# A gated FFT and MLP mixer on one core: first x block and last store in halves on two queues, two filter loads moved to GpSimd's queue

## The chip, the cores and the metric

One core of a Trainium2 chip runs the whole kernel. The metric is device time in microseconds (us), the median of several runs. The engines are TensorE (PE, with its weight loads as PEld), VectorE (DVE), ScalarE (ACT), GpSimd (POOL) and SyncE (SP). DMA transfers are issued here from three of them: SyncE, ScalarE and GpSimd; a "q" behind an engine's name in a profile row (SPq, ACTq, POOLq) is its instruction queue.

## The reference

The input x is 2048 rows (s) by 512 columns (d), bf16. Two branches are mixed by a gate per row:

```
g = sigmoid(sum_d x * gate_w)
a = irfft2( rfft2(x) * (w_r + 1j*w_i) )                 # w_r, w_i: 2048 x 257
h = layernorm over d of x
u = gelu( h^T w1 + b1 )                                  # w1: 2048 x 1792
b = (u w2 + b2)^T                                        # w2: 1792 x 2048
out = g * a + (1 - g) * b
```

## The kernel before

Rows are held as 16 blocks of 128 partitions, j = 4q + r: q is the quarter of the rows, r the residue of the row modulo 4. `x4` and `o4` are the views of x and of the output in that order; `t["x"]` is the tile `[128, q, r, 512]`. So "block 0 of x" is q = 0, r = 0.

**Stages.** (1) x, the first part of w1 and tables arrive. For each block there are statistics (VectorE's `bn_stats`, L489, or for blocks 8, 12, 5 and 2 ScalarE's sum and square, L499 and L503), then ScalarE's `rstd` (L493), then the normalised block `h` (VectorE L520 or ScalarE L550). (2) TensorE multiplies w1 by h, `m1` (L722), into 14 row tiles of u, and between them takes the forward transform along s (`fa`, L579 to L582, evicted by ScalarE at L585) and along d (`fb`, L687 and L690, evicted at L694). (3) VectorE multiplies the spectrum by the filter W (L827), and prepares single columns for it: `wprep` (L776 to L780) reads all of W, `c0a` (L790 and L791) copies one column of each half of the spectrum, `c0b` (L808 to L813) multiplies them, `nyq` (L800 to L803) does a single line. (4) TensorE multiplies w2 by gelu(u), `m2` (L988), and between those products takes the inverse transforms (L888 to L895, L970 to L974). (5) The two branches are added per pair of blocks (L993 to L1018), and for the last two blocks by L1030 straight from PSUM. Blocks are stored in groups: 0 to 3, 4 to 7, 8 to 11, 12 and 13, 14, 15. Block 15 is computed and stored in two parts of 384 and 128 columns.

**The order of work.** Every step is a task in a list, `add(engine, cost, emit, reads, writes, prio, ...)`. A planner (`Plan.order`) simulates the list with its own costs. Each time an engine is free it takes the ready task of lowest `prio`, and the tasks are emitted in the order of their planned starts; that gives each engine's instruction order. The planner reckons DMA as one stream that serves transfers in the order of issue. An issue from SyncE or ScalarE is held until the transfer eight before it has landed. `pk=(n, size, k)` gives a transfer's packets, their bytes, and how many of the 16 DMA engines take part. Tasks of the engine name "NOP" emit nothing and only carry dependencies. On the chip the instructions of an engine run in that order, each when its operands are there. All DMAs of the kernel's own helpers are issued at L317 (and the gathers at L462).

**What the change touches.**
- `ld_x0(q, eng, prio)` loads block q of r = 0 (128 rows of 1024 bytes). Block 0 goes on SyncE's queue, blocks 2, 1 and 3 on ScalarE's, ahead of ScalarE's first activation (`presq`, L372, with a table load). On SyncE the four pieces of w1 for r = 0 (`ld_w10`), the table `ta`, then x and w1 for r = 1, 2, 3 follow.
- `ld_W(comp, ...)` loads the filter, comp 0 from w_r and comp 1 from w_i, in five direct transfers and eight gathers. Transfers 0 and 1 are small and go on GpSimd's queue early. Transfers 2 (63 partitions, 252 rows of 514 bytes), 3 and 4 go on SyncE's queue behind w1. The gathers are GpSimd's; they stand behind `hold`, a copy of one element that waits for the last block of x.
- `store` writes a group; for block 15 it is called for n = 0 (384 columns) and n = 1 (128 columns).

Other steps that are spoken of: nine warm-up matmuls (L367) run on TensorE while the first data arrive; `ti` is the table of the inverse transform, loaded on GpSimd's queue behind the gathers; `wa` and `wb` are the buffers for w1 and later w2.

Of the kernel before, what the change touches and what calls it, by code (L numbers as in the profile page):

```python
# [143 lines left out]
class Plan:  # L144
# [11 lines left out]
    def add(self, eng, dur, emit, reads=(), writes=(), prio=0.0, alloc=(), free=(), pk=None, after=()):  # L156
        t = Task()
        t.eng, t.dur, t.emit, t.prio = eng, dur, emit, prio
        t.alloc, t.free, t.pk = tuple(alloc), tuple(free), pk
        t.users, t.end, t.ready = [], None, 0.0  # L160
        deps = set(after)
        for k in reads:
            if k in self.last_w:
                deps.add(self.last_w[k])
            self.readers.setdefault(k, []).append(t)
        for k in writes:
            if k in self.last_w:
                deps.add(self.last_w[k])
            deps.update(self.readers.get(k, ()))
            self.last_w[k] = t  # L170
            self.readers[k] = []
        deps.discard(t)
        t.deps = deps
        self.tasks.append(t)
        return t
# [100 lines left out]
def kernel(  # L276
# [13 lines left out]
    nc = tc.nc  # L290
    V, A, T = nc.vector, nc.scalar, nc.tensor
# [3 lines left out]
    x4 = A_x[0].rearrange(rows, q=4, r=4)  # L295
    o4 = out[0].rearrange(rows, q=4, r=4)
# [16 lines left out]
    add = pl.add  # L313
    t = {}

    def dma(out_ap, in_ap, eng=None):
        (eng or nc.sync).dma_start(out=out_ap, in_=in_ap)  # L317
# [34 lines left out]
    a0 = add("SP", 0.6, alloc_first, writes=["warm", "xs", "eps"], prio=-9)  # L352
# [7 lines left out]
    def ld(keys, dst, src, pk, prio, eng="SP"):  # L360
        return add(eng, 0.6 if eng == "POOL" else 0.43, lambda: dma(dst(), src, {"SP": None, "ACT": A, "POOL": nc.gpsimd}[eng]), writes=keys, prio=prio, pk=pk, after=[a0])
# [25 lines left out]
    def ld_x0(q, eng, prio):  # L387
        ld([("x", 0, q)], lambda q=q: t["x"][:, q, 0, :], x4[:, q, 0, :], (P, 1024), prio, eng)
# [5 lines left out]
    def ld_ta(r, prio, eng="SP"):  # L394
        ld([("ta", r)], lambda r=r: t["ta"][:, r, :], tabs["ta"][:, r, :], (P, 1280), prio, eng)

    ld_x0(0, "SP", -9)
    ld_x0(2, "ACT", -9)
    ld_w10(0, "SP", -8.9)
    ld_x0(1, "ACT", -8.9)  # L400
# [5 lines left out]
    for r in range(1, 4):  # L406
        for qs in ((slice(0, 2), slice(2, 4)) if r == 1 else (slice(0, 4),)):
            n = qs.stop - qs.start
            ld([("x", r, q) for q in range(4)[qs]], lambda r=r, qs=qs: t["x"][:, qs, r, :], x4[:, qs, r, :], (P * n, 1024), 2 * r + 0.1 * qs.start)
            add("SP", 0.43, ld_w1(r, qs), writes=[("w1", 0, 4 * q + r) for q in range(4)[qs]], prio=2 * r + 0.25 + 0.1 * qs.start,  # L410
                pk=(P * n, 1536))
# [27 lines left out]
    def ld_W(comp, pr, early):  # L439
        w = wsrc[comp]  # L440
        v = w.rearrange("(e c k) l -> c e k l", e=4, k=4)
        z = w.rearrange("(e h i n k) l -> n h k i e l", e=4, h=2, n=2, k=2)
        W = lambda: t["W"][:, comp]
        few = w.rearrange("(c b a w) l -> w c a b l", c=2, b=2, a=2)[0:1, 0]
        keys = []
        for n, (dst, src, pk) in enumerate((
                (lambda: W()[0:1, 0, :, 0, 0:257].rearrange("p (a b) l -> p a b l", a=2), few, (4, 514, 4)),
                (lambda: t["wn"][:, comp, 0:257], w[1024:1025, :], (1, 514, 1)),
                (lambda: W()[1:64, 0, :, 0, 0:257], z[0, 0, 0, 1:64], (252, 514, 9)),
                (lambda: W()[64:128, 0, :, 0, 0:257], z[1, 0, 0], (256, 514)),  # L450
                (lambda: W()[:, 1, :, 0, 0:257], v[:, :, 1, :], (512, 514)))):
            keys.append(("Wl", comp, n))
            add("SP" if n > 1 else "POOL", 0.5 if n > 1 else 0.55, lambda dst=dst, src=src, e=None if n > 1 else nc.gpsimd: dma(dst(), src, e),
                writes=keys[-1:], prio=pr + 0.1 * n if n > 1 else early + n, pk=pk, after=[a0])
        if comp == 0:
            def hold():
                nc.gpsimd.tensor_copy(t["hold"][:], t["x"][0:1, 3, 3, 0:1])
            add("POOL", 0.2, hold, reads=[("x", 3, 3)], writes=["hold"], prio=early + 19, after=[a0])
        for lt in range(2):
            for e in range(4):  # L460
                keys.append(("Wg", comp, lt, e))
                add("POOL", 1.0, lambda lt=lt, e=e: nc.gpsimd.indirect_dma_start(  # L462
                    out=W()[:, lt, e, 1, 0:257], out_offset=None, in_=w,
                    in_offset=bass.IndirectOffsetOnAxis(ap=t["ix"][:, 4 * lt + e:4 * lt + e + 1], axis=0)),
                    reads=["ix", "hold"], writes=keys[-1:], prio=early + 20, pk=(P, 514), after=[a0])
        add("NOP", 4.0, lambda: None, reads=keys, writes=[("W", comp)])
# [17 lines left out]
    for r in range(4):  # L484
# [10 lines left out]
        for n, j in enumerate(OWN[r]):  # L495
# [11 lines left out]
            else:  # L507
                add("DVE", 0.82, lambda j=j: stat(j), reads=[("x", r, j // 4)], writes=[("mv", j)], prio=pj, after=[n0] if j == 4 else ())
            sj = add("ACT", 0.28, lambda j=j: sq(t["rstd"][:, j:j + 1], t["mv"][:, j, 1:2], 1.0 / D if j in ASTAT else 1.0),
                reads=[("mv", j), "eps"], writes=[("rstd", j)], prio=-3)  # L510
# [153 lines left out]
    for lt in range(2):  # L664
        pr = 3.0 + 0.1 * lt
# [262 lines left out]
    for i in range(NW):  # L928
        n = (0, 3, 5)
# [31 lines left out]
    for grp in groups:  # L961
# [72 lines left out]
        for n, cs in enumerate(parts):  # L1034
            def store(grp=grp, cs=cs):
                q, r0, r1 = grp[0] // 4, grp[0] % 4, grp[-1] % 4 + 1
                dma(o4[:, q, r0:r1, cs], t["tb_"][:, grp[0]:grp[-1] + 1].rearrange("p j h d -> p j (h d)")[:, :, cs])
            add("SP", 0.5, store, reads=[("o", j) for j in grp] + [("of", j, n) for j in grp if j >= LATE], prio=50,
                pk=(P * len(grp), 2 * (cs.stop - cs.start)))

    order_ = pl.order()
# [33 lines left out]
```

## Time and profile before

| what | value |
|---|---|
| median of 3 runs | 130.48 us (130.34 to 130.52) |
| the profiled execution | 129.9 us, of which its span is 128.1 us |
| TensorE busy | 122.4 us, 96% of the span |
| VectorE busy | 109.9 us, 86% |
| ScalarE busy | 81.4 us, 64% |
| GpSimd busy | 26.4 us, 21% |
| granted TensorE clock | 1.0 in all 40 slices |
| DMA moved | 23.14 MB, mean 181 GB/s over the span |
| first real matmul starts | 5.17 us |
| last instruction of VectorE | 125.38 to 125.73 us |

Rows of the timeline give the start and the duration in us from the start of the span, the engine, the line of the kernel, the operation, the output and input tiles with their shapes, a count where rows were merged, and in brackets the idle time before it with what ended it. Rows of waits give who waited for whom, the total in us, how often, and the longest. Rows of DMA issues give output and input, the issuing queue, the count, the size, and the time from issue to landing. Busy time of PE is modelled: overlapping matmuls are each shown longer than the step from one to the next.

### The profile page before, as it was taken

Reading aid. Unit: us, or ns where it says so; the run is one execution under the profiler, and the core shown is the slowest. Engines: PE = TensorE matmul, PEld = TensorE weight load, DVE = VectorE, ACT = ScalarE, POOL = GpSimd, SP = SyncE. Lnnn points to the kernel's source line nnn. Section 1 sums busy time; section 2 is a strip of 40 time slices with the busy share of each in tenths; the row PEclk is TensorE's granted clock in tenths of the full one; section 3 lists DMA queues with packets and bytes.
Section 4 is the critical chain, followed back from the end, with each engine's and each line's share of the span. In section 5 each row is a group of like instructions: output and inputs, shape, how many; then the busy total and the mean of one; then the engine's idle time right before and its main releaser. Section 6 shows DMA issues by size and latency. Waiting matters only on the chain.

```text
span 128.1 us, 2101 instructions
## 1 busy us (share of the span) xinstructions
PE 122.4 (96%) x745; PEld 69.4 (54%) x759; DVE 109.9 (86%) x242; ACT 81.4 (64%) x170; POOL 26.4 (21%) x35
## 2 busy tenths in 40 slices
PE   6999889999999999999999999999999999999991
PEld 2455345655444467754445545556875676655570
DVE  2796989999999999889999999999586489999832
ACT  3879679797997899978220046225995599842200
POOL 5970005778978500000000000000000000000000
PEclk9999999999999999999999999999999999999999
DMA  3999999999999999980008800000000001243031
GB/s 102 345 333 383 319 394 382 352 339 338 257 188 214 347 409 411 416 338 26 0 0 298 360 0 0 0 0 10 0 0 0 0 5 67 97 164 155 14 123 41
DMA packets 15027, 23.14 MB, mean 181 GB/s; under 512 B 1464, under 2 KB 12106, under 8 KB 15018
## 3 DMA queue, kind: packets, MB, share of 16 engines
q1 hardware_dynamic: 13338, 19.70, 46.1%
q0 software_dynamic: 1200, 2.91, 7.4%
q10 hardware_dynamic: 480, 0.40, 0.9%
q8 instruction: 6, 0.10, 0.3%
q14 instruction: 3, 0.02, 0.1%
HBM read 20.90 MB, written 2.10 MB: 180 GB/s over the span
## 4 chain that ended last, share of the span: by engine, by line
PE 82%; DMA 11%; ACT 2%; issue 1%; ACTq 1%; SPq 0%; DVE 0%
PE acc L988 37%; PE acc L722 27%; DMA x<-in_A_x_dram 11%; PE fb L722 3%; PE fb L690 1%; PE fb L888 1%; PE fa L888 1%; PE fa L690 1%; PE fa L581 1%; PE fa L582 1%; ACTq L317 1%; ACT gl L503 1%; PE fa L988 1%; PE fa L579 1%; PE fb L687 1%
## 5 line engine op out<-in xcount | busy, mean ns | idle before, releaser
L988 PE MATMUL acc<-gl,wb 128*128 128x512 bf16 (+1 forms) x124 | 31.9, 376 | 0.2
L722 PE MATMUL acc<-h,wb 128*128 128x512 bf16 x124 | 28.9, 379 | 0.1
L988 PE MATMUL acc<-gl,wa 128*128 128x512 bf16 (+1 forms) x93 | 23.5, 376 | 0.1
L988 PEld LDWEIGHTS <-wb 128*128 128x128 bf16 x136 | 14.6, 114 | 10.6 <-issue 0.2
L1004 ACT ACTIVATE x<-acc,ombb,omg 128x512 bf16<-128x512 f32 x14 | 10.7, 780 | 14.6 <-PE acc L988 14.6
L722 PEld LDWEIGHTS <-wb 128*128 128x128 bf16 x128 | 12.5, 98 | 13.6
L722 PE MATMUL acc<-h,wa 128*128 128x512 bf16 (+1 forms) x66 | 16.8, 369 | 0.8 <-DMA wa<-in_B_w_dram 0.5
L988 PEld LDWEIGHTS <-wa 128*128 128x128 bf16 x102 | 11.2, 113 | 8.6
L722 PEld LDWEIGHTS <-wa 128*128 128x128 bf16 x102 | 9.9, 99 | 9.9 <-DMA wa<-in_B_w_dram 1.6
L742 ACT ACTIVATE gl<-acc,b1f 128x512 bf16<-128x512 f32 x12 | 8.1, 698 | 7.2 <-PE acc L722 7.2
L489 DVE BATCH_NORM_STATS2 stats<-x 128x6 f32<-128x512 bf16 x12 | 8.2, 686 | 3.1 <-DMA x<-in_A_x_dram 3.1
L758 ACT ACTIVATE x<-x 128x512 bf16<-128x512 bf16 x16 | 10.0, 637 | 0.0
L585 ACT CAST X<-fa 128x512 bf16<-128x512 f32 x16 | 8.8, 576 | 1.4 <-PE fa L582 1.4
L462 POOL DMA_INDIRECT W<-in_A_w_i_dram,ix x8 | 9.2, 1150 | 2.4 <-issue 2.4
L722 PE MATMUL fb<-h,wa 128*128 128x512 bf16 (+1 forms) x33 | 9.5, 366 | 0.0
L462 POOL DMA_INDIRECT W<-in_A_w_r_dram,ix x8 | 8.6, 1070 | 2.3 <-issue 2.3
L550 ACT ACTIVATE h<-x,nmr,rstd 128x512 bf16<-128x512 bf16 x8 | 6.5, 810 | 0.3 <-DVE nmr L547 0.3
L978 ACT ACTIVATE X<-fa,g 128x512 bf16<-128x512 f32 x8 | 5.7, 711 | 1.3 <-PE fa L974 1.3
L859 ACT CAST s<-fa 8x512 bf16<-8x512 f32 x1 | 0.6, 575 | 8.3 <-PE fa L857 8.3
L978 ACT ACTIVATE X<-fb,g 128x512 bf16<-128x512 f32 x8 | 5.7, 718 | 0.0
L694 ACT CAST B<-fa 128x512 bf16<-128x512 f32 x8 | 5.0, 630 | 0.2 <-PE fa L690 0.2
L694 ACT CAST B<-fb 128x512 bf16<-128x512 f32 x8 | 5.0, 626 | 0.0
(178 smaller groups left out, 244.1 us busy)
## 6 DMA issues: line engine op xcount, KB each, us to landing
wb<-in_B_w_dram SPq DMA_DIRECT2D x8, 512.0 KB, 9.8
wb<-in_B_w_dram SPq DMA_DIRECT2D x4, 1024.0 KB, 7.7
wa<-in_B_w_dram SPq DMA_DIRECT2D x3, 1024.0 KB, 11.3
wa<-in_B_w_dram SPq DMA_DIRECT2D x2, 768.0 KB, 11.6
out_dram<-x SPq DMA_DIRECT2D x3, 512.0 KB, 2.9
x<-in_A_x_dram SPq DMA_DIRECT2D x2, 512.0 KB, 11.8
wa<-in_B_w_dram SPq DMA_DIRECT2D x4, 192.0 KB, 3.8
wa<-in_B_w_dram SPq DMA_DIRECT2D x2, 384.0 KB, 6.5
```

The costliest lines, as they stand in the source:

```text
L462: add("POOL", 1.0, lambda lt=lt, e=e: nc.gpsimd.indirect_dma_start(out=W()[:, lt, e, 1, 0:257], out_offset=None, in_=w, in_offset=bass.Ind ...
L489: V.bn_stats(out=t["stats"][:, j, :], in_=t["x"][:, j // 4, j % 4, :])
L550: add("ACT", act(512, 2), lambda j=j: A.activation(t["h"][:, j // 4, j % 4, :], t["x"][:, j // 4, j % 4, :], ActF.Identity, bias=t["nmr"][ ...
L585: add("ACT", act(512), lambda r=r, dq=dq: A.copy(t["X"][:, :, r, :, dq, :], t["pa", r, dq][:]), reads=[("pa", r, dq)], writes=[("X", r, dq ...
L690: T.matmul(pb[:, :, 1::2, :], lhsT=w(k), rhs=tbl(k, c), start=(k == 2), stop=(k == 3))
L694: A.copy(t["B"][:, lt, e, 2 * c:2 * c + 2, :].rearrange("p s (i b) -> p s i b", b=4), t["pb", lt, e, c][:].rearrange("p s b i -> p s i b"))
L722: T.matmul(t["u", ft][:, cs], lhsT=w[:, j // 4, j % 4, c * P:(c + 1) * P], rhs=t["h"][:, j // 4, j % 4, cs], start=(j == jorder[0] and not ...
L742: gelus.append(add("ACT", act(512, 1), lambda ft=ft: A.activation(t["gl"][:, ft, :], t["u", ft][:], ActF.Gelu_apprx_tanh, bias=t["b1f"][:, ...
L758: A.activation(t["x"][:, q, r, :], t["x"][:, q, r, :], ActF.Copy, accum_out=t["glog"][:, 4 * q + r:4 * q + r + 1])
L978: A.activation(epair(j // 2 % NEO)[:, j % 2], t["i3", j][:], ActF.Copy, scale=t["g"][:, j:j + 1])
L988: T.matmul(t["y", j, n][:, cs], lhsT=w[:, o, 512 * q + r:512 * q + 512:4], rhs=t["gl"][:, ft, cs], start=(ft == 0), stop=(ft == NFT - 1))
L1004: A.activation(tbuf(j).rearrange("p h d -> p (h d)"), t["y", j, 0][:], ActF.Identity, bias=t["ombb2"][:, j:j + 1], scale=t["omg"][:, j:j + 1])
```

## The change

Block 0 of x is loaded in two transfers of 64 partitions, the first on SyncE's queue and the second on ScalarE's, both ahead of everything else there; a NOP task joins them. The third direct filter transfer (n = 2) of each component goes on GpSimd's queue instead of SyncE's, behind `hold`: for w_r between `hold` and its gathers, for w_i between the gathers of w_r and those of w_i. The store of block 15's last 128 columns is issued in two transfers of 64 partitions, the first from ScalarE and the second from SyncE.

```diff
-    ld_x0(0, "SP", -9)
+    for n, eng in enumerate(("SP", "ACT")):
+        ps_ = slice(64 * n, 64 * n + 64)
+        ld([("x0", n)], lambda ps_=ps_: t["x"][ps_, 0, 0, :], x4[ps_, 0, 0, :], (64, 1024), -9.1, eng)
+    add("NOP", 0.0, lambda: None, reads=[("x0", 0), ("x0", 1)], writes=[("x", 0, 0)])
     ld_x0(2, "ACT", -9)
     ld_w10(0, "SP", -8.9)
...
         keys = []
+        if comp == 0:
+            def hold():
+                nc.gpsimd.tensor_copy(t["hold"][:], t["x"][0:1, 3, 3, 0:1])
+            add("POOL", 0.2, hold, reads=[("x", 3, 3)], writes=["hold"], prio=early + 19, after=[a0])
...
-            add("SP" if n > 1 else "POOL", 0.5 if n > 1 else 0.55, lambda dst=dst, src=src, e=None if n > 1 else nc.gpsimd: dma(dst(), src, e),
-                writes=keys[-1:], prio=pr + 0.1 * n if n > 1 else early + n, pk=pk, after=[a0])
-        if comp == 0:
-            def hold():
-                nc.gpsimd.tensor_copy(t["hold"][:], t["x"][0:1, 3, 3, 0:1])
-            add("POOL", 0.2, hold, reads=[("x", 3, 3)], writes=["hold"], prio=early + 19, after=[a0])
+            add("SP" if n > 2 else "POOL", 0.5 if n > 2 else 0.55, lambda dst=dst, src=src, e=None if n > 2 else nc.gpsimd: dma(dst(), src, e),
+                reads=["hold"] if n == 2 else (), writes=keys[-1:], prio=pr + 0.1 * n if n > 2 else early + (19.5 if n == 2 else n), pk=pk, after=[a0])
...
-            add("SP", 0.5, store, reads=[("o", j) for j in grp] + [("of", j, n) for j in grp if j >= LATE], prio=50,
+            def store2(grp=grp, cs=cs):
+                q, r = grp[0] // 4, grp[0] % 4
+                for lo, eng in ((0, A), (64, None)):
+                    dma(o4[lo:lo + 64, q, r, cs], t["tb_"][lo:lo + 64, grp[0]].rearrange("p h d -> p (h d)")[:, cs], eng)
+            add("SP", 0.5, store2 if n == 1 else store, reads=[("o", j) for j in grp] + [("of", j, n) for j in grp if j >= LATE], prio=50,
                 pk=(P * len(grp), 2 * (cs.stop - cs.start)))
```

## The prediction

> **What bounds the kernel now.** I read the engine shares first, then who waited for whom on TensorE, then the order of time at three places: the start, the filter product, the end.
>
> ```profile
> PE 122.4 (96%) x745; PEld 69.4 (54%) x759; DVE 109.9 (86%) x242; ACT 81.4 (64%) x170; POOL 26.4 (21%) x35
> PE fa L367 <- DVE eps L329: 1.0, 1, 1.0
> PE acc L722 <- DMA wa<-in_B_w_dram: 0.5, 1, 0.5
> PE fa L579 <- ACT X L585: 0.5, 1, 0.5
> ...
> 5.17:20.00 14.83, 13.72 (x83) 7.57 (x84) 13.05 (x36) 11.56 (x33) 3.70 (x7) 1.00 1.04 361
> 20.00:66.00 46.00, 45.68 (x275) 24.82 (x280) 43.96 (x103) 37.57 (x86) 18.94 (x18) 1.00 0.88 273
> ```
>
> The first line is the page, the next three are all of TensorE's waits, the last two are busy time by stretch (span, then PE, PEld, DVE, ACT, POOL, then clock, DMA share, GB/s). After its warm-up TensorE waits twice: 0.5 us at 15.47 for a piece of w1, and 0.5 us at 19.40 for an eviction that stands behind the x block landing at 16.80. Up to 20 us the 16 DMA engines are full (share 1.04, 361 GB/s). From 20 on TensorE is full at clock 1.00. So the end is: DMA stream up to 19.40, a fixed queue of matmuls to 125.4, then a tail.
>
> The start, and the tail (start, duration, what; the DMA rows end in KB and us to landing):
>
> ```profile
> 2.15 1.28 ACT L372 ACT_TABLE_LOAD   x1 [2.15 <-issue]
> 3.41 0.69 DVE L489 BATCH_NORM_STATS2 stats<-x 128x6 f32<-128x512 bf16 x1 [1.84 <-DMA x<-in_A_x_dram]
> 3.65 0.61 ACT L499 ACTIVATE gl<-x 128x512 f32<-128x512 bf16 x1
> 4.36 0.29 ACT L493 ACTIVATE rstd<-mv,eps 128x1 f32<-128x1 f32 x1
> ...
> 122.32 0.75 DVE L1030 SCALAR_TENSOR_TENSOR x<-acc,omg,x 128x512 bf16<-128x512 f32 x1 [1.12 <-PE acc L988]
> 124.59 0.62 DVE L1030 SCALAR_TENSOR_TENSOR x<-acc,omg,x 128x384 bf16<-128x384 f32 x1 [1.53 <-PE acc L988]
> 125.38 0.35 DVE L1030 SCALAR_TENSOR_TENSOR x<-fa,omg,x 128x128 bf16<-128x128 f32 x1 [0.17 <-PE fa L988]
> out_dram<-x SPq DMA_DIRECT2D x1, 96.0 KB, 1.6
> out_dram<-x SPq DMA_DIRECT2D x1, 32.0 KB, 1.5
> ```
>
> ScalarE holds three x loads ahead of its table load; block 0 of x reaches VectorE at 3.41, its rstd runs at 4.36, the first real matmul at 5.17. At the end VectorE waits for TensorE, twice over a microsecond: it has slack. The last store is issued at 125.75, lands at about 127.25, and 0.85 us of closing follow to 128.1.
>
> **Part 1, block 0 of x in halves.** The first slice of 3.2 us moved 102 GB/s, 326 KB, the next ran at 345 GB/s, so data flows from about 3.2 - 326/345 = 2.25 (estimate). Today blocks 0 and 2 (262 KB) go side by side: through at 3.01, seen by VectorE 0.40 later. With only block 0 in front (131 KB) it is seen at 2.63 + 0.40 = 3.03; the other end is no gain, 3.41. ScalarE now issues four loads instead of three, 0.46 each: table load at 2.61, the first instruction after presq at 4.11 (3.65 + 0.46). VectorE's statistics take 0.95 (3.41 to 4.36), so rstd of block 0 can run at max(3.98, 4.11) = 4.11, if it goes ahead of block 8's sum (L499). In the planner's order it does, since block 2 of x moves behind half of block 0. From rstd to matmul takes 0.81: 4.92, but the nine warm-up matmuls end at 5.02. Gain: 0.15. In the old order of ScalarE rstd would stand at 4.82: a loss of 0.46. I take the gain.
>
> Behind it block 8 is later: sum from 4.31, square 5.05, rstd 5.88 (0.83 after, as today), normalised 6.21 to 6.61, matmul 6.7 against 6.65 now. TensorE's twelve half matmuls (1.48) end at 6.50, so 0.2 is lost again. Sum at 6.7: +0.05, bounds -0.15 and +0.46. All of it goes into the 0.5 us wait at 15.47, which the DMA stream sets. With that cover gone it would count in full.
>
> Does the stream move? Same bytes, same order on SyncE. Tile's transfers wait for the one eight before (w1's fourth piece starts at 3.59, 0.56 after ta: it waits for x). One more in front puts ta under that wait, 2.60 to about 3.1, and what follows up to 0.4 later; three w1 pieces (576 KB, 1.6 us) are then queued, so no engine runs dry. By bounds: 64 KB less ahead on SyncE's own queue, -0.18; the issue lag in full, +0.4. Taken: 0, as the stream is full.
>
> The Trainium skill speaks against this part: "DMA: Bandwidth & Descriptors", section "Rules for kernel authors", says that transfers to disjoint partition halves serialize on the same engines and one whole transfer should be used. By it block 0 would be seen at 3.41 as now and the 0.15 would fall away; the sum at the end stays.
>
> **Part 2, the filter loads.** GpSimd: hold ends at 20.71; two direct loads at 0.54 to 0.61 each (its rows), with up to the 0.30 that stands between its gathers: 1.1 to 1.8 us for what is queued behind, 16 gathers and the ti load. The last gather, issued at 42.24, landing 7.3 later at 49.5, comes at 50.6 to 51.3; VectorE first uses W at 54.31. Cover 3.0. The ti load moves from 43.22 to at most 45.0, lands 8.2 later, 53.2; TensorE reads it at 88.23. SyncE drops two transfers between 26.91 and 36.61, so w2 starts up to 3 us earlier, and is not used before 66.21. The 126.5 KB burst at 20.7 costs other loads 0.35 us: w1's last piece lands near 22.6 and is used after 24.3, the first wb loads land near 29.7 and are used at 33.31.
>
> What does move is VectorE's order, because the planner charges gathers issued behind w2 with w2's bytes. Worked through by hand, the filter counts as ready some 2 to 3 us later in its reckoning, and c0a of the second half (L790) slips in directly behind wprep. That copy needs the last spectrum eviction:
>
> ```profile
> 54.31 0.41 DVE L776 TENSOR_SCALAR W<-W 1x1028 bf16<-1x1028 bf16 x1
> 55.33 0.16 DVE L808 TENSOR_TENSOR cm<-c,wpm 128x8 f32<-128x8 f32 x1
> 58.06 0.15 DVE L790 CAST c<-B 128x8 f32<-128x8 bf16 x1
> 56.64 0.58 ACT L694 CAST B<-fb 128x512 bf16<-128x512 f32 x1
> ```
>
> The eviction ends at 57.22, so VectorE would stand from 55.4 to 57.25: a hole of 1.9. TensorE fills with the second layer's matmuls (L988), which need none of it; the inverse transform moves back with the plan. Tail: VectorE's own work for rows 14 and 15 ends at 119.30 and 120.59 and with it at 122.5; one L1018 (0.69) brings 123.2, L1030 of row 14 (0.75) 123.95, and row 15's is due at 124.59. Cover left: 0.65. Cost taken: 0; bounds 0 and +0.6 (hole one microsecond larger, then spread over the slack of 0.17 and up at each L1030).
>
> **Part 3, the last store.** 96 KB land in 1.6, 32 KB in 1.5: 64 KB are 0.1, so 16 KB save about 0.03. SyncE issues stores in 0.33; at the start ScalarE's issues took 0.41 to 0.45 beside SyncE's 0.39 to 0.43. Its half may land 0.02 to 0.12 later. Bounds -0.1 and +0.15; taken -0.03, nearest to the size rows.
>
> **Sum:** 0 + 0 - 0.03. The profiled execution took 129.9 (span 128.1 and 1.8 around it), 0.58 below the median of 130.48; its difference is carried over: 130.45.
>
> **The rivals.** *Slower: the hole outgrows its cover.* If the planner puts c0a even ahead of wprep (in its reckoning the two lie half a microsecond apart), the hole is 57.25 - 54.31 = 2.9. It decides from 2.6 on. Row 14's L1030 ends near 124.95, the next two follow 0.2 to 0.4 late, and its 128 KB store lies beside the last ones: +0.3 to +0.6, about 130.9. For it: VectorE at 86%. Against it: 1.1, 1.5 and 2.2 us waits of VectorE in the tail.
> *Faster: the early stream lands earlier.* If x and w1 on SyncE's queue gain the 64 KB (0.18) and both waits of TensorE shrink by that, with 0.1 at the store: -0.28, 130.2. For it: 1.0 us of TensorE's waiting hangs on that stream. Against it: share 1.04.
> *The change does not do what it says:* halves that share the engines arrive together with what they displaced, and 130.5 stays. It lies inside the forecast.
>
> **How the numbers follow.** Forecast, no change that counts: 0.42 (0.12 of it the last rival). Slower 0.31: 0.18 the hole, 0.13 the early order of ScalarE or the store's second queue past their covers. Faster 0.27. About 0.2% (0.26 us) is what a measurement of this kernel can tell from no change. The range goes from 129.9 (the faster rival with the store's bound and one full wait of 0.5) to 131.1 (the slower one at its upper price). The forecast's own range is 130.2 to 130.7.
>
> **What would show it.** Right: L489 first at about 3.05, the table load at 2.61, the first L722 near 5.0, a wait at 15.4 for wa and at 19.4 for ACT as now, L790 second pair before L808 with a wait of about 1.9, PE's last matmul near 125.3, stores landing near 127.2. Wrong: TensorE waiting anywhere after 20; L1030 of row 15 behind row 14's; the L722 start at 5.6; the x landing at 16.8 shifted by 0.3 or more.

## The result, and the profile after

The changed kernel took 131.39 us (median of 12 runs, 130.62 to 131.90), the kernel before in the same comparison 129.63 us (12 runs, 128.98 to 130.52). The paired ratio is 1.0119, 95% interval 1.0090 to 1.0148: 1.54 us slower, bounds 1.17 and 1.92 (the ratio times 129.6; the two medians differ by 1.76). The execution that was profiled took 130.62 us (span 128.8), the shortest of its twelve; so its trace shows only 0.7 of the 1.54 us, and the rest has to be looked for in the experiments. Five runs below (e5_store_act, e6_store_sp2, e7_x0_cols, e8_x0_sp2, e15_x0_merge) fell on chips that lowered the clock in some or all of their executions, and what is used of their times is from undisturbed executions alone.

Engine shares and all waits of TensorE, after (page, then chain of waits):

```profile
PE 122.5 (95%) x745; PEld 69.6 (54%) x759; DVE 110.3 (86%) x242; ACT 81.1 (63%) x170; POOL 28.7 (22%) x37
```
```profile
PE fa L367 <- DVE eps L329: 1.0, 1, 1.0
PE acc L725 <- DVE h L523: 0.8, 2, 0.4
PE fa L582 <- ACT X L588: 0.4, 2, 0.2
```

TensorE has the same work to 0.1 us, and its waits after the warm-up now sum to 1.2 instead of 1.0. But they lie elsewhere: 0.8 stand at the start (VectorE's `h`), 0.4 behind the eviction that was seen at 19.4 before. The wait for w1 at 15.47 is gone. The start, in order of time (start, duration, engine, what, and what it waited for):

```profile
0.75 2.45 ACTq L317 DMA_DIRECT2D x<-in_A_x_dram  x4
...
3.23 1.28 ACT L372 ACT_TABLE_LOAD   x1 [3.23 <-issue]
...
3.38 0.69 DVE L492 BATCH_NORM_STATS2 stats<-x 128x6 f32<-128x512 bf16 x1 [1.80 <-DMA x<-in_A_x_dram]
...
4.73 0.28 ACT L496 ACTIVATE rstd<-mv,eps 128x1 f32<-128x1 f32 x1
4.91 0.61 ACT L502 ACTIVATE gl<-x 128x512 f32<-128x512 bf16 x1
...
5.44 1.01 PE L725 MATMUL acc<-h,wa 128*128 128x256 bf16 x4 [0.42 <-DVE h L523]
...
6.46 0.69 DVE L492 BATCH_NORM_STATS2 stats<-x 128x6 f32<-128x512 bf16 x1 [0.79 <-DMA x<-in_A_x_dram]
6.50 0.29 ACT L496 ACTIVATE rstd<-mv,eps 128x1 f32<-128x1 f32 x1
...
7.29 0.40 DVE L523 TENSOR_SCALAR h<-x,mv,rstd 128x512 bf16<-128x512 bf16 x1
...
7.74 1.02 PE L725 MATMUL acc<-h,wa 128*128 128x512 bf16 x4 [0.41 <-DVE h L523]
```

Block 0 of x is seen at 3.38, where it was 3.41. ScalarE's four issues fill 2.45 us, where three took 1.37; the table load stands at 3.23 instead of 2.15, the first matmul at 5.44 instead of 5.17, the 512-wide matmuls of block 8 at 7.74 instead of 6.65.

Two things make block 8 late. ScalarE starts later, so block 8's rstd runs at 6.50 (5.39 before). And VectorE has the statistics of block 4 ahead of block 8's `h`: they waited 0.79 us for block 4's x, up to 6.46 (5.20 before, without a wait), and `h` follows them at 7.29 (6.03 before). By the trace's records of the transfers' semaphores block 8's x landed at 4.68 (3.57 before) and block 4's at 6.44 (4.90): each stands one place further back on ScalarE's queue.

The transfers themselves start later (busy by stretch; the last columns are clock, DMA share and GB/s):

```profile
2.00:3.00 1.00, 1.00 (x4) 0.30 (x2) 0.00 (x0) 0.84 (x1) 1.00 (x3) 1.00 1.04 271
...
0.00:16.00 16.00, 14.25 (x70) 6.90 (x72) 11.73 (x34) 11.43 (x28) 7.47 (x17) 1.00 0.89 296
```
```profile
2.00:3.00 1.00, 1.00 (x4) 0.30 (x2) 0.00 (x0) 0.00 (x0) 1.00 (x3) 1.00 0.82 157
...
0.00:16.00 16.00, 13.95 (x67) 6.88 (x69) 11.50 (x33) 11.23 (x28) 7.50 (x17) 1.00 0.88 285
```

From 2 to 3 us 157 GB/s were moved instead of 271, and over the first 16 us 285 instead of 296 (294 to 306 in the profiles below whose start is that of the kernel before). On SyncE's queue `ta` is issued at 3.37 (2.60 before), the next x transfer at 4.69 (3.96):

```profile
3.37 0.33 SPq L317 DMA_DIRECT2D rot<-dft_ta  x1
3.75 0.43 SPq L317 DMA_DIRECT2D wa<-in_B_w_dram  x1
4.69 0.90 SPq L317 DMA_DIRECT2D x<-in_A_x_dram  x2
```

The filter product and the tail on VectorE, with the last store's half on ScalarE's queue:

```profile
55.39 0.17 DVE L793 CAST c<-B 128x8 f32<-128x8 bf16 x1 [1.00 <-ACT B L697]
55.88 0.17 DVE L794 CAST c<-B 128x8 f32<-128x8 bf16 x1 [0.32 <-ACT B L697]
55.99 0.42 DVE L779 TENSOR_SCALAR W<-W 1x1028 bf16<-1x1028 bf16 x1
```
```profile
122.92 0.74 DVE L1033 SCALAR_TENSOR_TENSOR x<-acc,omg,x 128x512 bf16<-128x512 f32 x1
...
124.66 0.62 DVE L1033 SCALAR_TENSOR_TENSOR x<-acc,omg,x 128x384 bf16<-128x384 f32 x1 [0.99 <-PE acc L991]
...
125.44 0.35 DVE L1033 SCALAR_TENSOR_TENSOR x<-fa,omg,x 128x128 bf16<-128x128 f32 x1 [0.16 <-PE fa L991]
125.83 0.57 ACTq L317 DMA_DIRECT2D out_dram<-x  x1
```
```profile
out_dram<-x ACTq DMA_DIRECT2D x1, 16.0 KB, 2.1
```

The two copies c0a (L793, L794) went ahead of wprep (L779) and waited 1.32 us for the eviction; wprep runs 1.68 us later than before. The tail has absorbed it: row 14 is 0.6 later, row 15 starts at 124.66 where it was 124.59, and still waits 0.99 for TensorE. The last VectorE instruction ends 0.06 later than before (125.79 against 125.73). What follows it, to the end of the span, took 3.05 us instead of 2.39: the store's half took 0.57 to issue and 2.1 to land, where one store of 32 KB took 0.33 and 1.5.

### The profile page after: what moved, and what is told of

The parts are those of the page before. It is cut to its first block, busy times and chain, and to the rows that moved or that the text cites. A ratio compares the mean times of both kernels' runs of the same rounds, so it can differ in the third digit from the quotient of the medians.

```text
span 128.8 us, 2103 instructions
## 1 busy us (share of the span) xinstructions
PE 122.5 (95%) x745; PEld 69.6 (54%) x759; DVE 110.3 (86%) x242; ACT 81.1 (63%) x170; POOL 28.7 (22%) x37
## 4 chain that ended last, share of the span: by engine, by line
PE 82%; DMA 11%; ACT 2%; ACTq 1%; issue 1%; DVE 0%
PE acc L991 37%; PE acc L725 26%; DMA x<-in_A_x_dram 11%; PE fb L725 3%; PE fb L891 1%; ACTq L317 1%; PE fa L693 1%; PE fa L891 1%; PE fb L693 1%; PE fa L584 1%; PE fa L585 1%; ACT gl L506 1%; PE fa L991 1%; PE fa L582 1%; PE fb L690 1%
## 5 line engine op out<-in xcount | busy, mean ns | idle before, releaser
L465 POOL DMA_INDIRECT W<-in_A_w_r_dram,ix x8 | 9.4, 1181 | 2.4 <-issue 2.4
```

## The experiments

Every kernel below is the kernel before with only the edit shown. Ratios are paired with runs of the kernel before on the same chip; a per cent is 1.3 us.

**One part at a time.** The edits are the three hunks of the change.

e1_x0, the halves of x block 0 alone. Expected:

> Only block 0 of x in halves; filter and store as before. Theory A (the start carries most of the loss: ScalarE holds four issues, the changed kernel's trace shows 0.60, 0.86, 0.44 and 0.44 instead of 0.46 each, so the table load is 1.1 us later, block 8's matmuls are 1.1 us later, and the 0.5 us wait for the DMA stream hides only part): +0.6 to +1.0 us, table load near 3.2, first real matmul near 5.4. Theory B (the DMA stream hides all of the start, as predicted): within 0.2 us. The profiled pair of traces, whose last VectorE instruction is only 0.06 us later, speaks for B; the medians, which differ by 1.5 us where this pair of executions differs by 0.7, for A.

e2_store, the halves of the last store alone. Expected:

> Only the last store in halves on ScalarE's and SyncE's queues. Theory A (a transfer of 64 partitions issued beside another costs more to issue and lands later: 0.57 instead of 0.33 and 2.1 instead of 1.5 us in the changed kernel's trace): +0.5 to +0.7 us, all after the last VectorE instruction. Theory B (my prediction): within 0.15 us.

e3_filter, the filter loads alone. Expected:

> Only the third filter transfer of each component on GpSimd's queue. Theory A (VectorE's later wprep is covered by the slack of 0.6 us at the end, and the transfers are off the path): within 0.2 us, wprep near 56.0 and behind the second c0a, TensorE without a wait after 20. Theory C (the filter is the hidden loss, in executions other than the profiled one): +0.4 to +1.0 us, seen as a late L1030 for block 14 or 15.

Measured: e1_x0 131.03 us, ratio 1.0087 (1.0053 to 1.0120); e2_store 131.00, 1.0089 (1.0055 to 1.0123); e3_filter 130.09, 1.0019 (0.9995 to 1.0042). Parts 1 and 3 each cost about 1.1 us, more than theory A gave either of them, and part 2 nothing that this comparison can tell from zero. e3's VectorE order is not the one that its own expectation gave but the one that the prediction had worked out by hand (wprep, the first copy, then a wait):

```profile
54.80 0.41 DVE L776 TENSOR_SCALAR W<-W 1x1028 bf16<-1x1028 bf16 x1
...
55.87 0.17 DVE L790 CAST c<-B 128x8 f32<-128x8 bf16 x1
57.74 0.17 DVE L791 CAST c<-B 128x8 f32<-128x8 bf16 x1 [1.69 <-ACT B L694]
```

The wait was 1.69, and L790 and L791 of the second half are behind wprep; in the whole change they are ahead of it. Neither order moved the end measurably.

In e1's profiled execution TensorE waited more than in the kernel after:

```profile
PE fa L582 <- ACT X L588: 1.7, 2, 1.0
...
PE acc L725 <- DVE h L523: 0.9, 2, 0.5
```

x's third residue (ScalarE's fourth sum) was there at 18.03 instead of 16.80. This execution is the longest of e1's nine (131.88), and such figures vary without any change at the start: in the kernel before and in e2, e3, e4 and e5b, whose start is the same, the third residue came at 16.61 to 17.29, the waits behind the warm-up sum to 1.0 to 2.3, and the last matmul starts at 124.92 to 125.61. e1 lies outside with 18.03, 2.6 and 126.68; the kernel after (16.76, 1.2, 125.19) does not.

e13_x0_store, parts 1 and 3 together (both hunks as in e1 and e2). Expected:

> The change without its filter part. If the parts add: +1.7% (0.9 and 0.9), which would mean that the filter part gains 0.5% in the company of the others. If all three are near the 1.2% of the change with the filter at 0 to 0.2%: +1.0 to +1.3%.

Measured: 131.80, 1.0162 (1.0121 to 1.0203). The two parts add: 0.87% and 0.89%. It also leaves the whole change, 1.0119, below its two costly parts, by 0.4% with some 0.5% of uncertainty; whether the filter loads give anything back in company stays open, and the next finding takes away part of the difference.

**What the store pays for.** Four ways of writing the last 32 KB:

```diff
 e4_store_cols   2 x (128 partitions x 64 columns), ScalarE and SyncE
 e5_store_act    1 x (128 x 128), on ScalarE's queue
 e6_store_sp2    2 x (64 partitions x 128 columns), both on SyncE
-                for lo, eng in ((0, A), (64, None)):
-                    dma(o4[lo:lo + 64, q, r, cs], t["tb_"][lo:lo + 64, grp[0]]...[:, cs], eng)
+                for c, eng in ((cs.start, A), (cs.start + 64, None)):            # e4
+                    dma(o4[:, q, r, c:c + 64], t["tb_"][:, grp[0]]...[:, c:c + 64], eng)
+                dma(o4[:, q, r, cs], t["tb_"][:, grp[0]]...[:, cs], A)           # e5
+                for lo, eng in ((0, None), (64, None)):                          # e6
```

> The last store in two transfers on the same two queues, but of 128 partitions and 64 columns each instead of 64 partitions and 128 columns. If two queues issuing at the same moment is what costs, the issue is again near 0.57 and the loss as in the run with the store alone (+0.5 to +0.7 us). If the 64 partitions are what costs, the issues are near 0.33 to 0.4 and the time is within 0.2 us of before.

> The last store whole, in one transfer of 128 partitions, but on ScalarE's queue instead of SyncE's. Theory P (64 partitions are what costs: the column halves issued in 0.37 and 0.33 and landed in 1.6, the partition halves in 0.54 to 0.57 and 1.8 to 2.1): issue near 0.37, tail after VectorE's last instruction 2.4 to 2.8 us as with one store on SyncE, time within 0.2 us of before. Theory Q (a store on ScalarE's queue costs in itself, which would explain why the column halves were still 0.5% slower): tail 2.8 us or more, +0.4 to +0.7 us.

> The last store in two transfers of 64 partitions, both on SyncE's queue, ScalarE's left alone. Theory P: each issue near 0.55, one behind the other, so the second starts 0.6 us late and lands late: +0.8 to +1.2 us, tail 3.2 us or more. Theory Q: issues near 0.33, +0.2 to +0.4 us.

> Once more the last store whole on ScalarE's queue. Theory P (64 partitions cost, not the queue): within 0.3 us of before, issue near 0.37, tail 2.4 to 2.8 us. Theory Q: +0.4 us or more.

Measured: e4_store_cols 130.57, 1.0052 (1.0022 to 1.0081). e5_store_act 0.9955 (0.9901 to 1.0008); repeated as e5b_store_act 129.68, 1.0009 (0.9983 to 1.0034). e6_store_sp2 1.0107 (1.0052 to 1.0163); its two issues took 0.58 and 0.59, one behind the other. The landings of ScalarE's part in e4, e5b and, for comparison, e2:

```profile
out_dram<-x ACTq DMA_DIRECT2D x1, 16.0 KB, 1.6
```
```profile
out_dram<-x ACTq DMA_DIRECT2D x1, 32.0 KB, 1.5
```
```profile
out_dram<-x ACTq DMA_DIRECT2D x1, 16.0 KB, 1.8
```

ScalarE's queue costs nothing (e5b: issue 0.37, landing 1.5). Two transfers cost little at the landing, as long as each has 128 partitions (e4: 1.6). The 64 partitions do: from the issue to the moment at which SyncE's wait for the landing passes, the trace has 1.48 us before, 1.44 in e4 (SyncE's part; ScalarE's landed 1.58 after its issue), 1.51 in e5b, and 2.07 in e2, 2.07 after, 2.08 in e13 (the later of the two halves). By the records of the packets the first data packet leaves 0.83 after the issue before and in e4, but in the kernel after 1.22 after the issue for one half and 1.49 for the other.

Why then is e4 0.5% slower? Its trace gives the larger part of the answer. At the end SyncE waits for the transfers' semaphores, two in an instruction, in a fixed order; the views leave semaphore instructions out, so these rows are from the trace's records (start in us, what SyncE waits for):

```
before                        e1_x0 (whole store, split x)   after
126.13  S114, S113            127.69  S114, S113             126.43  S114, S113
126.20  S99,  S112            128.79  S99,  S112  <- store   126.49  S99,  S112
126.26  S101, S111            128.85  S101, S111             126.56  S101, S111
126.32  S103, S110            128.91  S103, S110             126.62  S103, S110
126.38  S104, S109            128.97  S104, S109             126.68  S104, S109
126.44  S105, S108            129.03  S105, S108             126.74  S105, S108
126.50  S106, S107            129.10  S106, S107             126.97  S106, S107
126.87  S116, S100            129.15  S115, S100             127.90  S115, S100  <- store
127.23  S117, S115  <- store  129.22  S116, S117             127.96  S116, S117
128.11  end                   130.10  end                    128.84  end
```

The transfers of SyncE's and ScalarE's queues take eight semaphores in turn. The kernel before has 48 of them, and the last store has the eighth, whose wait is the last of the list: the others have run out while the store was in flight. With 49 (e1, e2, e4, e6, e7, e8, e14) it, or one half of it, has the first, S99, and seven waits of 0.06 stand behind it: 0.43 us that have nothing to do with how a transfer is cut. From the last wait of the list to the end of the span it is 0.88 in all three. The whole change has 48 again (one more for x, one more for the store, two filter loads fewer) and pays 0.06. So the single parts e1 and e2 look 0.43 us worse than they are in company: about 0.70 us (1.13 - 0.43) and 0.73 (1.16 - 0.43), of which the landing explains 0.59. e4 needs 1.87 from the issue to the last wait of the list, 0.39 more than before; 0.68 - 0.39 = 0.29 is left, which its interval (0.29 to 1.05, less the 0.39) no longer tells from zero. e3, with 46, pays 0.12; e13, with 50, whose halves have S101 and S99, pays 0.43.

**What the x halves pay for.** The same pieces of x block 0 in other forms:

```diff
-        ps_ = slice(64 * n, 64 * n + 64)
-        ld([("x0", n)], lambda ps_=ps_: t["x"][ps_, 0, 0, :], x4[ps_, 0, 0, :], (64, 1024), -9.1, eng)
+        cs_ = slice(256 * n, 256 * n + 256)                                       # e7: 128 partitions x 256 columns
+        ld([("x0", n)], lambda cs_=cs_: t["x"][:, 0, 0, cs_], x4[:, 0, 0, cs_], (P, 512), -9.1, eng)
-    for n, eng in enumerate(("SP", "ACT")):
+    for n, eng in enumerate(("SP", "SP")):                                        # e8: 64-partition halves, both on SyncE
```

> Block 0 of x in two transfers on SyncE's and ScalarE's queues as in the change, but of 128 partitions and 256 columns each. Theory S (the loss is a DMA stream that starts late: in the second from 2 to 3 us it moved 157 and 162 GB/s with the partition halves, 271 to 289 without; x and w1 then land later, and the matmuls with them): with quick issues (0.40 to 0.46) the stream starts as before, 250 GB/s or more from 2 to 3 us, table load near 2.6, time within 0.3 us of before. Theory T (the loss is ScalarE's fourth issue, which makes the table load and block 8 late): +0.4 to +1.0 us with the table load still late.

> Block 0 of x in two transfers of 64 partitions, both on SyncE's queue; ScalarE has its three loads as before. Theory S: SyncE's issues are near 0.55 to 0.6 each, w1 starts 0.7 us later, the stream is slow from 2 to 3 us (below 240 GB/s), and the time is +0.4 to +1.0 us although the table load is back at 2.15. Theory T: with the table load at 2.15 the time is within 0.2 us of before.

> Once more block 0 of x in column halves of 128 partitions on the two queues, since all executions of its first try ran at a granted clock of 0.95 to 0.98 and can't be compared. That profile's start can be read: issues of 0.39 and 0.46, table load at 2.64, first matmul at 4.88, but only 176 and 180 GB/s in the two microseconds from 2 to 4 (rows of 512 bytes). Theory S (the late stream is the loss): +0.4 to +1.0 us although the first matmul is early. Theory T (the late table load): within 0.3 us of before.

> Once more block 0 of x in halves of 64 partitions, both on SyncE's queue, for the same reason. Its profile showed issues of 0.6 each, the table load at 2.14, and 295 then only 134 GB/s from 2 to 4 us. Theory S: +0.7 to +1.5 us. Theory T: within 0.3 us, unless block 0 itself comes so late (statistics at 5.3) that its matmuls are late: then up to +1 us by either, with TensorE's waits before 9 us telling which.

The first tries (146.11 and 142.19 us) say nothing of the time. Repeated: e7b_x0_cols 130.85, 1.0074 (1.0042 to 1.0106); e8b_x0_sp2 132.77, 1.0217 (1.0153 to 1.0281). ScalarE's start in e7b:

```profile
0.75 1.86 ACTq L317 DMA_DIRECT2D x<-in_A_x_dram  x4
...
2.64 1.28 ACT L372 ACT_TABLE_LOAD   x1 [2.64 <-issue]
...
5.06 0.63 ACT L502 ACTIVATE gl<-x 128x512 f32<-128x512 bf16 x1 [0.52 <-DMA x<-in_A_x_dram]
...
7.46 1.02 PE L725 MATMUL acc<-h,wa 128*128 128x512 bf16 x4 [0.37 <-DVE h L523]
```

With 128 partitions the four issues take 1.86, 0.46 each, and the table load stands at 2.64: what the prediction had worked out for the halves (2.61). SyncE's first packet leaves at 1.77, as before (1.79); with 64 partitions it is 2.11 to 2.13, in e1, e13 and the kernel after. So the 64-partition form costs issue time and 0.34 us ahead of the first byte. But e7b gains nothing by that: block 8's own x is not there before 5.06, and its matmuls start at 7.46 all the same. Of e7b's 0.96 us, 0.43 are the closing list and another 0.16 stand between the list and the end; the 0.37 left, with 0.4 of uncertainty, decides for neither theory. In e8b, where no queue but SyncE's changes, ScalarE is early (table load 2.14), and block 0 is late:

```profile
5.47 0.69 DVE L492 BATCH_NORM_STATS2 stats<-x 128x6 f32<-128x512 bf16 x1 [3.89 <-DMA x<-in_A_x_dram]
...
7.14 1.01 PE L725 MATMUL acc<-h,wa 128*128 128x256 bf16 x4 [2.12 <-DVE h L523]
```

Two halves on one queue were together at 5.47, 2.1 us later than whole. By the records of the semaphores the first half landed at 3.62 and the second, issued at 1.39, at 5.37. It stood second on SyncE's queue, where the kernel before has w1's first piece, which was issued at 1.19 and landed at 4.67: a second place costs that much without halves too. e8b's loss, 2.8 us, is above both theories; TensorE, which waits for nothing behind this point, worked at half pace up to 12.84 (last section), and that adds to it.

**Which of the two delays counts, ScalarE's start or the stream?** Two kernels were meant to move only ScalarE's start, two only the stream. e10_act_late puts two loads of 128 x 16 bytes, which nothing uses, on ScalarE's queue behind its three; e11_act_only puts four copies of 128 columns, which nothing uses, behind ScalarE's first activation and changes no transfer.

```diff
+    for n in range(2):                                                            # e10
+        ld([("scr", n)], lambda n=n: t["scr"][:, 8 * n:8 * n + 8], x4[:, 0, 0, 0:8], (P, 16), -8.87, "ACT")
     def presq():
         A.activation(t["ombb2"][:, 0:1], t["eps"][:], ActF.Abs_reciprocal_sqrt, ...)
+        for _ in range(4):                                                        # e11
+            A.copy(t["gl"][:, 0, 0:P], t["warm"])
```

> The kernel before with two extra tiny loads (128 rows of 16 bytes into a scratch tile, 4 KB in all) on ScalarE's queue between its x loads and its table load: the table load moves from 2.15 to about 3.05, as in the change, and the byte stream stays. Theory S: within 0.3 us of before (block 8's matmuls late, hidden in the waits for the stream). Theory T: +0.6 to +1.0 us.

> The kernel before with four copies of 128 columns on ScalarE behind presq (of zeros, into a place that is overwritten later): ScalarE's first sum starts about 0.9 us later (near 4.6 instead of 3.65), no transfer and no order is changed. Theory T (the late ScalarE is the loss of block 0's halves): +0.6 to +1.0 us. Theory S (the late stream is): within 0.3 us, block 8's matmuls 0.5 to 0.9 us later, and the waits near 15 and 19 us shorter by as much.

e10_act_late: 131.32, 1.0130 (1.0077 to 1.0183). It is confounded: the second tiny load was issued only at 3.52, when the transfer eight before it (block 8's x) had landed, so the table load came at 3.88 and not at 3.05; two more transfers also held SyncE's issues back, with 210 and 206 GB/s from 6 to 8 us, and the closing list cost 0.37. e11_act_only: 130.83, 1.0076 (1.0047 to 1.0105), with the stream as before (299 GB/s from 2 to 3 us, 298 over 16) and no wait of TensorE but one:

```profile
PE acc L724 <- DVE h L522: 1.3, 1, 1.3
```
```profile
3.66 1.27 ACT L374 COPY gl<-xp 128x128 bf16<-128x128 bf16 x4
...
4.96 0.63 ACT L501 ACTIVATE gl<-x 128x512 f32<-128x512 bf16 x1
...
6.30 1.01 PE L724 MATMUL acc<-h,wa 128*128 128x256 bf16 x4 [1.27 <-DVE h L522]
...
7.24 0.40 DVE L522 TENSOR_SCALAR h<-x,mv,rstd 128x512 bf16<-128x512 bf16 x1
...
8.81 1.62 PE L724 MATMUL acc<-h,wa 128*128 128x512 bf16 x4
```

ScalarE 1.3 us late puts block 8's matmuls at 8.81, 2.16 later than before; the waits that stood after them (1.0) are gone, and 2.16 - 1.0 = 1.16 is the span's increase (129.2 - 128.1 = 1.1). So a late ScalarE alone can lead to a loss of this size, but in e11 it has help that the kernel after has not: block 8's `h` was ready at 7.64 (the row at 7.24), no later than there (7.69), and TensorE took it only 1.17 later, still working through block 0's matmuls at half pace (last section). Without that, as an estimate from these rows, 2.16 - 1.17 = 0.99 would have been left, no more than the 1.0 of waits covers.

The other way round, take bytes off the early stream. GpSimd loads `tb`, `gw` and `tg` (582 KB) at 7 to 9 us. e9_defer puts all three behind `hold` (20.12 before), e12_defer2 only `gw` and `tg` (288 KB). The lines of e12, with `load` taught to pass `reads` on:

```diff
-    load("gw", [P, D], BF16, gate_w[None, :].to_broadcast([P, D]), (P, 1024), prio=28.3, eng="POOL")
+    load("gw", [P, D], BF16, gate_w[None, :].to_broadcast([P, D]), (P, 1024), prio=29.3, eng="POOL", reads=[("x", 3, 3)])
...
-    load("tg", [P, 642], BF16, tabs["tg"], (P, 1284), prio=60, eng="POOL")
+    load("tg", [P, 642], BF16, tabs["tg"], (P, 1284), prio=60, eng="POOL", reads=[("x", 3, 3)])
```

> The kernel before with three loads of GpSimd's queue (tables tb and tg and the gate weights gw, 582 KB) moved from about 8 us to behind hold, at 20 us and later. Theory S: 582 KB at 361 GB/s are 1.6 us of stream ahead of x and w1; block 2 of the third residue lands about 1 us earlier than 16.8, TensorE's wait at 19.4 shrinks, and the time is -0.4 to -1.0 us. Theory T: the start of ScalarE is unchanged, so within 0.2 us.

> The kernel before with only gw and tg (288 KB) moved behind hold on GpSimd's queue; the bias table tb stays early. Theory S: 288 KB at 361 GB/s are 0.8 us of stream, the x block of the third residue lands near 16.0 instead of 16.6 to 17.3, TensorE's wait at 19.4 mostly goes: -0.4 to -0.8 us. Theory T: within 0.2 us.

e9_defer: 130.90, 1.0104 (1.0043 to 1.0166). x's third residue is there at 14.55, 2.25 earlier, but TensorE's bias product (L701) needs `tb` and stands at 31.61 instead of 22.65:

```profile
PE acc L722 <- ACT gl L742: 2.4, 1, 2.4
```

The gain turned into a new wait. e12_defer2: 128.25, 0.9890 (0.9852 to 0.9927), 1.4 us faster than the kernel before and so the best here. x's third residue is there at 15.06, and of TensorE's waits only the one ahead of the warm-up is left:

```profile
PE fa L367 <- DVE eps L329: 1.0, 1, 1.0
```

This bears out the prediction's first reading: 1.0 us of waits hung on the early stream, and without them the end comes down by as much or more (1.4, bounds 0.9 and 1.9).

e14_x0_on_defer puts e1's hunk on e12's kernel, where no wait is left for a late start to hide in. Expected:

> The kernel with the two late GpSimd loads (gw and tg moved behind the hold, 1.1% faster than before), and on top of it the first block of x as two 64-partition halves. In that kernel TensorE waited for nothing after its start, so there is no slack left for a late start to hide in. Theory (the halves start block 8's matmuls 0.8 to 1.5 us later, and the waits of 1.0 us after them covered part of it): the lateness now counts in full, 1.0 to 1.5 us over that kernel, a ratio to before of 0.997 to 1.001. Rival (the loss is the slower stream alone, and the start is covered by something else): with x(2) already landing about 2 us earlier the halves cost at most 0.3 us, a ratio of 0.989 to 0.992.

130.02, 1.0024 (0.9996 to 1.0051): 1.0024 / 0.9890 is 1.35% or 1.75 us more than e12. The closing list has 0.43 of it, and 1.3 is left, against 0.70 for the same halves on the kernel before. The rival falls; but the 1.3 and the 0.70, with 0.6 and 0.4 of uncertainty, are not told apart, so that the cover is not shown by them. Nor does the run part the two delays as it was meant to: in its profiled execution (131.68, the longest of its twelve) x's third residue came at 17.32, 2.26 later than in e12, with 1.6 us of waiting for it.

e15_x0_merge keeps the halves and joins two of w1's first pieces, so that there are as many transfers in front as before:

```diff
-    ld_w10(2, "SP", -8.8)
-    ld_w10(1, "SP", -8.7)
+    add("SP", 0.4, ld_w1(0, slice(1, 3)), writes=[("w1", 0, 4), ("w1", 0, 8)], prio=-8.8, pk=(2 * P, 1536), after=[a0])
```

> The x halves alone, and two of w1's first pieces (for x blocks 1 and 2, 192 KB each) joined into one transfer, so that the number of transfers in front is that of before again. A transfer waits for the one eight before it, and with the halves the one that waits first (ta) was issued at 3.37 us instead of 2.60, the next x transfer at 4.69 to 5.30 instead of 3.96. Theory (one more transfer in front holds the stream back): ta is issued at 2.6 to 2.9, the following x transfer at 4.0 to 4.4, x's third residue lands near 16.8, TensorE waits at most 0.6 us for the eviction behind it. ScalarE stays late (table load at 3.2, block 8's matmuls near 7.5), and the ratio to before falls from 1.0087 to 1.003 to 1.006. Rival (the 64-partition transfers themselves hold the stream back, whatever their number): the issues on SyncE stay 0.7 us or more late, the third residue lands after 17.4, and the ratio stays at 1.007 to 1.011.

Its time (145.85 us) is of no use, so the ratios that were expected stay untested. But the granted clock is 1.0 from 4.46 to 35 us, and the start can be read:

```profile
2.45 0.47 SPq L317 DMA_DIRECT2D rot<-dft_ta  x1
3.36 0.33 SPq L317 DMA_DIRECT2D wa<-in_B_w_dram  x1
3.73 1.93 SPq L317 DMA_DIRECT2D x<-in_A_x_dram  x2
```

`ta` is issued at 2.45, the next x transfer at 3.73: a little earlier than before (2.60 and 3.96) and than the theory had it, where e1 has 3.29 and 5.08. In e1 the issue of `ta` carries a wait for the semaphore of ScalarE's half of block 0, which landed at 3.27; in e15 it carries none. So it is the number of transfers that held SyncE's `ta` back (a transfer waits for the one eight before it). The second x transfer is late still, 5.29 (4.92 before): it waits for block 8's x, which landed at 5.27. The other effect stays: 160 GB/s from 2 to 3 us (e7b, with whole partitions and half rows, has 196), table load at 3.20, block 8's matmuls at 7.69; x's third residue came at 17.12, between theory and rival and within what an unchanged start gives. With 48 transfers the last store is again the last of the closing list, and 0.88 lie between the list and the end.

## Why the prediction was wrong, step by step

It said 130.45, no change, with a range up to 131.1, and had everything on the path as covered or nil; 131.39 was measured. Its reading of the bound holds: waits at the start, a fixed queue of TensorE, a tail. Three terms were mis-sized: ScalarE's start with what follows it up to block 8, the stream, and the store. ScalarE's issues and the store rest on one assumption, that half a transfer costs no more to issue and to land than a whole one.

- **Part 1, ScalarE's issues and block 8.** Taken as 0.46 for one more; the halves made it 1.08 (0.60 and 0.86 for the first two, 0.44 for the others). The order of ScalarE that it chose came true, with rstd ahead of block 8's sum, at 4.73 instead of 4.11. "Block 0 seen at 3.03" was wrong: 3.38 (and data flows from 1.79 before, by the packets, not from 2.25). The chain "sum from 4.31 ... normalised 6.21" left out two things: when the x of blocks 8 and 4 lands, one place further back on ScalarE's queue (4.68 and 6.44, where it was 3.57 and 4.90), and that VectorE has block 4's statistics ahead of block 8's `h`. The gain of 0.15 was a loss of 0.27 at the first matmul; block 8's matmuls came at 7.74 and not 6.7, a term of +1.09 instead of +0.05, over twice its upper bound of 0.46. The nearest rival is "early order of ScalarE past its cover", which had 0.13 together with the store; but it was not the order that failed.
- **Its cover.** It was put at 0.5, the wait at 15.47; the waits came to 1.0. In the profiled execution 0.6 of them went, and TensorE's queue behind block 8 took 0.4 less (no row was found for that; at 27 us the matmuls of both kernels stand at the same time, 26.97 and 27.00), so the 1.09 did not reach the end. In the executions profiled of e1, e13 and e14 it did: behind block 8 TensorE still waited 1.7, 0.7 and 1.6, since the stream that makes these waits is later too (third residue at 18.03, 17.48 and 17.32).
- **"No engine runs dry … taken: 0, as the stream is full."** `ta` was worked out for 3.1 and issued at 3.37, and what follows 0.7 to 1.1 late (after, e1) instead of "up to 0.4". The engines were at 157 to 171 GB/s from 2 to 3 us in all kernels with the 64-partition halves on two queues (269 to 299 with the whole block), and x's third residue came at 16.76 to 18.03 (16.61 to 17.29 with an unchanged start). e1 has 1.7 us of waiting where 0.5 stood; e4, with an unchanged start, has 1.8 there, so this figure alone proves nothing.
- **Part 3, the landing.** Worked out from sizes alone at -0.03, bounds -0.1 and +0.15; it measures +0.59 at the landing. The size rows (96 KB 1.6, 32 KB 1.5) say nothing of the number of partitions, and that is what was halved. ScalarE's queue, which the prediction suspected, is free (e5b).
- **Part 2** was right: 0, with the hole on VectorE of the predicted kind (1.69 in e3 against 1.9), the last gather issued at 44.68 instead of 42.24 within its cover, and the tail's slack taking it up. In the whole change c0a went ahead of wprep, the slower rival's order; its price didn't come, since the hole was 1.32 and not 2.9, and VectorE still waited 0.99 for TensorE at row 15.
- **The Trainium skill's rule** that two transfers to disjoint partition halves serialize and aren't worth it ("DMA: Bandwidth & Descriptors", section "Rules for kernel authors") was cited and got 0.12, as the last rival. By it the 0.15 would have fallen away, and the trace agrees (3.38 against 3.41); its advice was right by more than it says, since the halves were not merely useless but cost issue and landing time.
- **Not in the prediction at all:** the closing list. In the change it is worth 0.06; in experiments that take one part alone it is worth 0.43, and would have been read as the part's price.

Added up: landing 0.59, list 0.06, x halves 0.70 (e1 less its list), filter 0.13 (e3 less its list, not told from zero) make 1.48, against 1.54 measured (1.17 to 1.92); the x halves and the filter carry some 0.4 and 0.3 of uncertainty, so that the close fit is in part luck. How the 0.70 divides between ScalarE and the stream is not settled. In the execution profiled of the kernel after, an estimate from the rows: had block 4's x been there, block 8's rstd (6.50 to 6.79) would have let its matmuls start near 7.25, so 0.6 of the 1.09 are ScalarE's start and 0.5 the stream. In e1, e13, e14 and e15 block 8's own x landed at 5.06 to 5.68, when ScalarE was already free. The stream's lateness has two causes (the number of transfers for SyncE's later issues, the form for the first microsecond).

## What to carry to other kernels

Price a transfer by its partitions and its place in the queue, not by its bytes, and ask of everything that moves back a place when it lands: look in the trace for a transfer of the same form, and if there is none, say so and take a wide bound. A wait that covers a delay covers it only if the delay doesn't also move what made the wait; ask that of every cover. And when one part of a change is tested alone, count the transfers: a part that changes their number can move a cost at the other end of the kernel, so compare the closing as well as the stage.

## What the runs showed of the hardware that was not expected

- A transfer of 64 partitions takes longer to issue than one of 128: 0.56 to 0.60 for x and 0.54 to 0.59 for the store, against 0.39 to 0.41 and 0.33 to 0.37; the issue behind it on ScalarE took 0.69 to 0.86 (0.44 before). Its first packet leaves 0.34 to 0.39 later, and that of the store's second half 0.66.
- TensorE starts at half pace, and the moment at which it goes to full pace differs from execution to execution. The "granted clock 1.0 in all 40 slices" of the page hides it: the trace has no clock record before 5.55 us in the kernel before and 6.34 in the kernel after, and where there is none the views print 1.00. Up to the first record 512-wide matmuls (the nine of the warm-up) follow one another by 0.43 us and 256-wide ones by 0.21; behind it by 0.215 and 0.11. The first record stands at 10.01 in e11 and at 12.84 in e8b, after 1.27 and 2.12 us without work, and at 3.81 to 6.97 in all others. An idle stretch does not do it alone: in e10, where the record (3.93) came ahead of 1.69 us without work, the twelve 256-wide matmuls behind them ran at full pace, 0.11 each; in e11 they took 2.51 us in all, where the kernel before took 1.48. This is why ScalarE's 1.3 us became 2.16 in e11. The Trainium skill ("TensorE: Matmul & The Clock Gate", section "What's actually happening") tells of a gate that opens after a busy window of some 3.4 us, in windows independent of the kernel's start; the 3.7 us (e11) and over 5 us (e8b) of half pace after the restart, and a moment that moves by 3 us between kernels with the same warm-up, go with that.
- 288 KB loaded at 8 us that could as well come after 18 us (no wait came of it) cost 1.4 us at the end (e12; bounds 0.9 and 1.9).
- The place of the last store in the closing list of semaphore waits is worth up to 0.43 us of 130, and the number of transfers on SyncE's and ScalarE's queues, anywhere in the kernel, sets it.
